# Third group of m's columns in the accumulators' banks, six g pairs parked in float32, and a maximum over partitions without a diagonal

## The chip, the cores and the metric

The program runs on one core of one Trainium2 chip. The metric is device time in microseconds of one execution of the whole program; smaller is better. The core has five engines that run at the same time, each through its own instruction list in order: TensorE (PE, matmuls; its weight loads are shown as PEld), VectorE (DVE), ScalarE (ACT), GpSimd (POOL) and SyncE (SP), which here only issues DMAs. They wait for each other by semaphores.

## The reference

```python
# q, k, v: (1, 6016, 256); tau = 1; C = 256, N = 6016
qn = q / (norm(q, axis=1) + 1e-6);  kn = k / (norm(k, axis=1) + 1e-6)
s = kn.transpose(0, 2, 1) @ qn / tau            # 256 x 256, contracted over the 6016 rows
a = softmax(s)                                  # over the last axis
x = v @ a                                       # 6016 x 256
h = x @ moe_w_in                                # 6016 x 2048
g = h * sigmoid(1.702 * h)
x = g @ moe_w_out                               # 6016 x 256
gate = sigmoid(x @ w_gate);  val = x @ w_val    # 6016 x 1536 each
out = (gate * val) @ moe2_w_out                 # 6016 x 256
```

The weights come as float64.

## The kernel before, in words

Everything is computed transposed: columns of v, h, g and y run along the free axis in 12 blocks of 512 tokens (the last one is shorter).

**Head of the program.** q and k are read in chunks; PE adds up the 256 x 256 scores in banks 0 and 1 of PSUM, the two accumulator banks (`ACC_BANK`). The norms, the softmax and a transpose give `et`. The weight w_in (256 x 2048, tile `full_in`, in four pieces of 512 columns) is turned from float64 words into float32: ACT takes the magnitude (line 503) and a sign (521), DVE shifts it (509) and joins the low bits (515), and GpSimd multiplies the sign in (525); ACT sums squares of a piece between shift and join (481), from which the piece's scale comes. w_out (called o1, tile `big`) goes the same way, since `BY_POOL` names "in" and "o1".

**m.** Softmax and w_in are folded into one matrix m = a @ w_in. Its 2048 columns come in four groups of 512, each in two halves: `m_unit` issues two float32 products (`L942`; four instructions in the profile) into one bank; ACT writes the float16 high part (`L312`, m_t<-ps), DVE the low part (`L315`, m_t<-ps). The scale `rss` of both comes from the maximum of w_in over all partitions: `p2_ops` builds a 128 x 128 diagonal of each partition's own maximum (`L281`, eye_b), multiplies it by ones on PE (`L285`) and takes the maximum of a row on DVE (`L288`, p_win; p_v is the same for block 0 of v, p_wo for o1).

**h and g.** An h unit (b, u) is a pair of 128-row tiles of h for block b (u = 0 to 7). In blocks 0 and 1 it is 12 float16 matmuls of 512 columns (`eight`: three products for each of 2 x 2 blocks) into a pair of PSUM banks; from block 2 on it is seven half-size products (`seven`, line 1031), which need sums of blocks of m (`m_sums`). For blocks 0 and 1 ACT then takes the gelu of both banks into a float32 tile gf (`L1175`), ACT or DVE makes the float16 high part gh (`L312` or `L1192`), and DVE the low part gl (`L315`). The tile gf has three buffers. gh and gl have three buffers (names gh, gl), and steps 3 to 11 have nine more (`room()`, shown as s_t) in memory that the head no longer needs.

**y.** A y unit multiplies a pair's gh and gl by w_out (tile `wo`, in high and low parts made by `L312` and `L315`, wo<-big) and adds into the accumulator banks (`L1007` to `L1009` with wo). So h units can run before w_out is ready, and y units can't.

**Order.** `Plan.run` is a list scheduler in the build: each operation has a cost, a rank (its number plus `plan.delay`) and its dependencies, and the scheduler writes out each engine's list. `ax_pair` hands out two pairs of PSUM banks in turn (4 and 5, 6 and 7) to units of m and h units; banks 2 and 3 serve `p2_ops` and later the seven products, banks 0 and 1 the scores and later y. On the chip each engine keeps the written order whatever happens. The lines on m, h and y at the program's end are

```python
M_FIRST, M_EVERY = 4, 1
m_units(M_FIRST)
        if b == 0 and u % 2 == 0:
            m_units((u // 2 + 1) * CC - m_next)
        h_unit(b, u, x - NG if NG <= x < NG + n_slots else None)
        if b == 0 and u % M_EVERY == M_EVERY - 1:
            m_units(CC)
        queue.append(step)
        if len(queue) > LAG:
            y_unit(*queue.pop(0))
```

Of the kernel before, what the change touches and what calls it, by code (L numbers as in the profile page):

```python
# [9 lines left out]
F32 = mybir.dt.float32  # L10
# [6 lines left out]
P = 128  # L17
# [3 lines left out]
LAG = 2  # L21
M_FIRST, M_EVERY = 4, 1
SUMS_AT = (1, 0), (1, 2), (1, 4), (1, 6)
# [5 lines left out]
S_AT = (73, 75, 86, 97)  # L29
BY_POOL = ("in", "o1")  # L30
LOOSE = ("in", "o1", "g", "v", "o2")

V0_DELAY, O1_DELAY, O1_SPLIT, SUM_FIRST = -105, 80, -20, 60

# [130 lines left out]
def fused_kernel(ctx, tc, q, k, vt, tau, w_in, w_o1, w_g, w_v, w_o2, outt):  # L165
# [93 lines left out]
    def p2_ops(name, amax, r, w, pe, before=(), after=()):  # L259
# [19 lines left out]

        def diagonal(e):  # L280
            nc.vector.tensor_scalar_mul(eye_b, T["ident_b"], own)  # L281

        def rows(e):
            T[kp] = bank(kp)
            nc.tensor.matmul(T[kp][:, :P], T["ones_b"], eye_b, start=True, stop=True)  # L285

        def top(e):
            nc.vector.tensor_reduce(out=p2, in_=T[kp][:, :P], axis=AX.X, op=ALU.max)  # L288

        op(diagonal, ("dve", 0.13), r=[k_own, ("ident_b",)], w=[("eye_b",)], lone=True)  # L290
        op(rows, ("pe", 0.1), r=[("eye_b",)], w=[kp])
        op(top, ("dve", 0.2), r=[kp], w=[w], lone=True)
        return p2

    def s_ops(name, p2, r, w, after=(), top=TOP):
# [4 lines left out]
        return s  # L300

    eye_b = small.tile([P, P], BF16, name="eye_b")

# [238 lines left out]
    def w_max(name, after=()):  # L542
# [26 lines left out]
        elif w_src[name][1]:  # L569
# [76 lines left out]
    def prepare(e):  # L646
        first["ones"] = sm_p.tile([P, P], F32, name="ones")
        nc.vector.memset(first["ones"], 1.0)
        T["ones_b"] = small.tile([P, P], BF16, name="ones_b")
        nc.vector.tensor_copy(T["ones_b"], first["ones"])  # L650
        first["k"] = sm_p.tile([P, TACC, C], F32, name="kacc")
# [278 lines left out]
    def m_unit(u):  # L930
# [4 lines left out]
        if i == 0:  # L935
            m_banks[fg] = ax_pair()
        kp = m_banks[fg][i]
# [191 lines left out]

    def h_unit(b, u, slot):  # L1130
        n = blocks[b][1]
# [4 lines left out]
        if u == 0:  # L1136
# [11 lines left out]
            for x, fn in enumerate((scale, inverse, shift)):  # L1148
                op(fn, ("dve", 0.07), r=[("vp2", b), ("sgin",)] + ([sk] if x else []), w=[sk])
        kf = ring("gf")  # L1150

# [21 lines left out]
        def both(e):  # L1173
            T[kf] = t_p.tile([P, 2 * NB], F32, tag="gf", name="gf" + name)
            nc.scalar.activation(  # L1175
                out=T[kf].rearrange("p (x n) -> p x n", x=2)[:, :, :n], in_=pair_ap(kx, n), func=AF.Gelu_apprx_sigmoid,
                scale=T[sk][0],
            )
# [20 lines left out]
        if b < PLAIN:  # L1199
            op(both, ("act", 0.12 + 1.02 * f), r=[kx, ka, sk], w=[kf], after=[t_op])  # L1200
            r = [kf, sk]
        else:
            op(lambda e: act(e, 0), ("act", 0.12 + 0.51 * f), r=[kx, ka, sk, kf], w=[("gf0", name)], after=[t_op])
            op(lambda e: act(e, 1), ("act", 0.12 + 0.51 * f), r=[kf, ("val2", kf), sk], w=[("gf1", name)], after=[t_op])
            r = [kf, ("gf0", name), ("gf1", name), sk]
        op(hi, [("act", 0.14 + 0.93 * f), ("dve", 0.1 + 0.53 * f, GH_DVE)], r=r, w=[k_g],
           after=before_m if slot == 0 else ())
        op(lo, ("dve", 0.12 + 1.14 * f), r=r + [k_g], w=[("glo", name)])
        g_keys[b, u] = k_g

# [125 lines left out]
    for x, step in enumerate(steps):  # L1336
        b, u = step
        if b == 0 and u % 2 == 0:
            m_units((u // 2 + 1) * CC - m_next)
        h_unit(b, u, x - NG if NG <= x < NG + n_slots else None)  # L1340
        if b == 0 and u % M_EVERY == M_EVERY - 1:
            m_units(CC)
        if step in SUMS_AT:
            m_sums(SUMS_AT.index(step))
        queue.append(step)
        if len(queue) > LAG:
            y_unit(*queue.pop(0))
# [171 lines left out]
```

## Time and profile before

| | |
|---|---|
| median of 3 runs | 1055.97 us (1055.26 to 1057.82) |
| the profiled execution | 1055.93 us, of which the span from the first to the last instruction is 1053.8 us |
| PE busy | 1038.5 us (99%), 7169 matmuls |
| PEld / DVE / ACT / POOL busy | 715.5 / 795.1 / 703.1 / 39.5 us (68% / 75% / 67% / 4%) |
| mean granted TensorE clock | 0.998 |
| share of PE in the chain that ended last | 92% |

Busy time is the sum of the instructions' times on an engine; a matmul's recorded time includes the passage of its last columns, so that neighbours overlap and a busy PE may still not be at its peak. The chain that ended last is followed back from the last instruction through whatever released each step. The three runs lie within 0.25% of each other.

### The profile page before, as it was taken

Reading aid. Unit: us, or ns where it says so; the run is one execution under the profiler, and the core shown is the slowest. Engines: PE = TensorE matmul, PEld = TensorE weight load, DVE = VectorE, ACT = ScalarE, POOL = GpSimd, SP = SyncE. Lnnn points to the kernel's source line nnn. Section 1 sums busy time; section 2 is a strip of 40 time slices with the busy share of each in tenths; the row PEclk is TensorE's granted clock in tenths of the full one; section 3 lists DMA queues with packets and bytes.
Section 4 is the critical chain, followed back from the end, with each engine's and each line's share of the span. In section 5 each row is a group of like instructions: output and inputs, shape, how many; then the busy total and the mean of one; then the engine's idle time right before and its main releaser. Section 6 shows DMA issues by size and latency. Waiting matters only on the chain.

```text
span 1053.8 us, 18271 instructions
## 1 busy us (share of the span) xinstructions
PE 1038.5 (99%) x7169; PEld 715.5 (68%) x7169; DVE 795.1 (75%) x1457; ACT 703.1 (67%) x1388; POOL 39.5 (4%) x43
## 2 busy tenths in 40 slices
PE   8989999999999999999999999999999999999998
PEld 6733456666666666666677777777777777777776
DVE  6988989989898766757686776767767667676665
ACT  6788467777867656656566666666666666666665
POOL 0232000000000000000000000000000000000000
PEclk9999999999999999999999999999999999999999
DMA  9930213210000000000000000000000000000000
GB/s 344 401 103 21 81 40 140 101 60 22 21 1 21 21 1 16 1 2 1 2 1 2 21 2 21 16 7 21 2 21 21 1 21 1 22 21 2 21 21 16
DMA packets 14518, 43.64 MB, mean 41 GB/s; under 512 B 1504, under 2 KB 2784, under 8 KB 12768
## 3 DMA queue, kind: packets, MB, share of 16 engines
q1 hardware_dynamic: 14432, 42.47, 11.2%
q8 instruction: 56, 0.92, 0.4%
q14 instruction: 30, 0.25, 0.1%
HBM read 36.31 MB, written 6.16 MB: 40 GB/s over the span
## 4 chain that ended last, share of the span: by engine, by line
PE 92%; DVE 2%; issue 2%; DMA 2%; ACT 1%; POOL 1%; SPq 0%; DVEq 0%; ACTq 0%; POOLq 0%
PE ps L1031 47%; PE ps L1009 14%; PE ps L1007 14%; PE ps L1008 14%; DMA m_t<-in_q 2%; PE ps L942 1%; PE ps L745 0%; POOL big L525 0%; DVE full_in L515 0%; POOL full_in L525 0%; PE ps L682 0%; DVE big L515 0%; DVE m_t L315 0%; ACT gh L312 0%; ACT m_t L1040 0%
## 5 line engine op out<-in xcount | busy, mean ns | idle before, releaser
L1031 PE MATMUL ps<-vo,s_t 128*128 128x256 f16 (+1 forms) x3024 | 371.0, 270 | 0.6 <-ACT m_t L1040 0.6
L1031 PEld LDWEIGHTS <-s_t 128*128 128x128 f16 x3024 | 292.7, 98 | 91.2 <-issue 1.0
L1045 DVE TENSOR_TENSOR gf<-ps,m_t 128x256 f32<-128x256 f32 (+1 forms) x448 | 184.8, 415 | 143.5 <-PE ps L1031 104.4
L1040 ACT COPY m_t<-ps 128x256 f32<-128x256 f32 (+1 forms) x448 | 162.3, 364 | 94.8 <-PE ps L1031 93.5
L1031 PE MATMUL ps<-vo,m_t 128*128 128x256 f16 (+1 forms) x1680 | 217.4, 270 | 0.4 <-ACT ps L1040 0.2
L1031 PEld LDWEIGHTS <-m_t 128*128 128x128 f16 x1680 | 162.6, 98 | 67.4 <-issue 1.5
L1393 ACT ACTIVATE gf<-ps,sgb 128x512 f32<-128x512 f32 (+1 forms) x144 | 97.5, 677 | 67.3 <-PE ps L1031 67.3
L1411 DVE TENSOR_TENSOR gl<-gf,gh 128x512 f16<-128x512 f32 (+1 forms) x144 | 97.8, 680 | 45.1 <-ACT gh L1406 42.4
L1009 PE MATMUL ps<-gh,wo 128*128 128x512 f16 (+1 forms) x348 | 130.2, 374 | 0.7 <-DVE wo L315 0.7
L1007 PE MATMUL ps<-gh,wo 128*128 128x512 f16 (+1 forms) x348 | 130.2, 374 | 0.7 <-ACT wo L312 0.7
L1008 PE MATMUL ps<-gl,wo 128*128 128x512 f16 (+1 forms) x348 | 130.2, 374 | 0.0
L1406 ACT CAST gh<-gf 128x512 f16<-128x512 f32 (+1 forms) x131 | 79.8, 609 | 72.0 <-PE ps L1009 71.8
L315 DVE SCALAR_TENSOR_TENSOR gl<-gf,sgi,gh 128x1024 f16<-128x1024 f32 (+1 forms) x87 | 110.2, 1269 | 4.0 <-ACT gh L312 3.6
L1399 DVE SCALAR_TENSOR_TENSOR gf<-gf 128x512 f32<-128x512 f32 (+1 forms) x144 | 98.0, 680 | 13.6 <-ACT gf L1393 0.7
L1008 PE MATMUL ps<-gl,wo_h 128*128 128x512 f16 (+1 forms) x288 | 107.9, 375 | 0.0
L1009 PE MATMUL ps<-gh,wo_l 128*128 128x512 f16 (+1 forms) x288 | 107.9, 375 | 0.0
L1007 PE MATMUL ps<-gh,wo_h 128*128 128x512 f16 (+1 forms) x288 | 107.9, 375 | 0.0
L1040 ACT COPY ps<-ps 128x256 f32<-128x256 f32 (+1 forms) x224 | 82.0, 367 | 16.8 <-PE ps L1031 15.7
L1192 DVE TENSOR_SCALAR gh<-gf,sgi 128x1024 f16<-128x1024 f32 (+1 forms) x64 | 49.0, 768 | 27.6 <-PE ps L1009 22.0
L1009 PEld LDWEIGHTS <-wo 128*128 128x128 f16 x384 | 37.6, 98 | 44.7 <-DVE wo L315 1.2
L1169 ACT ACTIVATE gf<-gf,sgs 128x512 f32<-128x512 f32 (+1 forms) x80 | 56.2, 709 | 14.4 <-DVE gf L1045 13.6
L1169 ACT ACTIVATE gf<-ps,sgs 128x512 f32<-128x512 f32 (+1 forms) x80 | 53.8, 673 | 11.1 <-PE ps L1031 10.7
(212 smaller groups left out, 999.7 us busy)
## 6 DMA issues: line engine op xcount, KB each, us to landing
v_raw<-in_vt SPq DMA_DIRECT2D x11, 512.0 KB, 3.9
out_t<-ob SPq DMA_DIRECT2D x22, 256.0 KB, 2.0
m_t<-in_k SPq DMA_DIRECT2D x9, 512.0 KB, 7.2
m_t<-in_q SPq DMA_DIRECT2D x9, 512.0 KB, 8.0
s_t<-in_w_o SPq DMA_DIRECT2D x3, 1024.0 KB, 4.9
s_t<-in_w_g SPq DMA_DIRECT2D x3, 1024.0 KB, 4.8
s_t<-in_w_v SPq DMA_DIRECT2D x3, 1024.0 KB, 4.9
big<-in_w_in SPq DMA_DIRECT2D x2, 1024.0 KB, 9.1
```

The lines of the kernel that those rows point to most:

```text
L315: nc.vector.scalar_tensor_tensor(out=lo, in0=x, scalar=s, in1=h, op0=ALU.mult, op1=ALU.subtract)
L1007: nc.tensor.matmul(ps[:, :n], w_h, x_h, start=first, stop=False)
L1008: nc.tensor.matmul(ps[:, :n], w_h, x_l, start=False, stop=False)
L1009: nc.tensor.matmul(ps[:, :n], w_l, x_h, start=False, stop=last)
L1031: nc.tensor.matmul(dst, l, r, start=start and y == 0, stop=y == 2, skip_group_check=True)
L1040: op(lambda e: nc.scalar.copy(out=dst, in_=bank(key)[:, :w]), ("act", 0.1 + w / 1150), r=[key], w=[wk], after=after)
L1045: nc.vector.tensor_add(val(half), bank(kw)[:, :w], other)
L1169: nc.scalar.activation(out=dst, in_=pair_ap(kx, w) if x == 0 else dst, func=AF.Gelu_apprx_sigmoid, scale=T[sk][0])
L1393: nc.scalar.activation(out=T[kf][:, :n].rearrange("p (x w) -> p x w", x=2), in_=pair_ap(kx, w), func=AF.Sigmoid, scale=T[sk])
L1399: nc.vector.scalar_tensor_tensor(out=v, in0=v, scalar=VSHIFT, in1=T[kf][:, :n], op0=ALU.mult, op1=ALU.mult)
L1406: nc.scalar.copy(out=T[name][0][:, :n], in_=T[kf][:, NB : NB + n])
L1411: nc.vector.tensor_sub(T[name][1][:, :n], T[kf][:, NB : NB + n], T[name][0][:, :n])
```

## The change

Four edits, and what follows from them in the written order.

1. **Banks of m.** Six units of m are issued ahead of the first h unit instead of four (`M_FIRST`), and the third group (fg == 2) goes to the accumulator banks 0 and 1 instead of a pair from `ax_pair`. The maximum of o1 moves from bank 0 to bank 3.
2. **Parked g.** For six h units, steps 3 to 8, that is (0,3) to (0,7) and (1,0), the gelu is written into float32 space of the late tiles y_f, wo_h and wo_l (`parked`) instead of the gf buffers; the high and low parts of these have a rank that is 60 later (`PARK_BY`).
3. **The maximum.** The diagonal and the tile of ones go. The own maximum of each partition, read as bfloat16 and broadcast along the columns, is the weight operand, and the identity is multiplied by it.
4. **o1 without GpSimd, and ranks.** o1 leaves `BY_POOL`: its sign is now joined by a second DVE operation (line 512 in the new file) in place of ACT's sign (521) and GpSimd's product (525), for each of four pieces. The maximum, scale and split of v's block 1 get a rank 60 earlier (`V1_DELAY`), and each `m_sums` stands behind the first product of its step.

```diff
-M_FIRST, M_EVERY = 4, 1
+M_FIRST, M_EVERY = 6, 1
...
-BY_POOL = ("in", "o1")
+BY_POOL = ("in",)
...
+V0_DELAY, V1_DELAY, O1_DELAY, O1_SPLIT, SUM_FIRST = -105, -60, 80, -20, 60
+PARK, PARK_BY = 6, 60
...
-        def diagonal(e):
-            nc.vector.tensor_scalar_mul(eye_b, T["ident_b"], own)
-
         def rows(e):
+
             T[kp] = bank(kp)
-            nc.tensor.matmul(T[kp][:, :P], T["ones_b"], eye_b, start=True, stop=True)
+            left = own.bitcast(BF16)[:, 1:2].broadcast_to([P, P])
+            nc.tensor.matmul(T[kp][:, :P], left, T["ident_b"], start=True, stop=True)
...
-            {"in": ("acc", 3), "o1": ("acc", 0)}.get(name), before, after,
+            {"in": ("acc", 3), "o1": ("acc", 3)}.get(name), before, after,
...
         if i == 0:
-            m_banks[fg] = ax_pair()
+
+            m_banks[fg] = ACC_BANK if fg == 2 else ax_pair()
...
+    def parked(i):
+
+        if i < YX:
+            return late_pools()["y"][:, i * 2 * NB : (i + 1) * 2 * NB]
+        return late_pools()["o2"][i - YX].bitcast(F32)[:, : 2 * NB]
...
-        kf = ring("gf")
+        kf = ring("gf") if park is None else ("gfp", park)
...
-            T[kf] = t_p.tile([P, 2 * NB], F32, tag="gf", name="gf" + name)
+            T[kf] = t_p.tile([P, 2 * NB], F32, tag="gf", name="gf" + name) if park is None else parked(park)
...
+        plan.delay = 0 if park is None else PARK_BY
         op(hi, [("act", 0.14 + 0.93 * f), ("dve", 0.1 + 0.53 * f, GH_DVE)], r=r, w=[k_g],
...
-        h_unit(b, u, x - NG if NG <= x < NG + n_slots else None)
+        h_unit(b, u, x - NG if NG <= x < NG + n_slots else None, x - NGF if NGF <= x < NGF + PARK else None)
...
-            m_sums(SUMS_AT.index(step))
+            m_sums(SUMS_AT.index(step), [step_op[step]])
...
+            plan.delay = V1_DELAY if b == 0 and fn in (v_max, v_scale, v_split) else 0
             fn(*args, after=[step_op[step]])
+            plan.delay = 0
```

On PE, from the transposes' end to the first h unit, the order before is this (two rows of `L942` are one unit of m; `own_v`, `own_win` and `eye_b` belong to the maxima of v's block 0 and of w_in):

```order
L942 MATMUL ps<-full_in,et 128x512 x6
L285 LDWEIGHTS ones_b
L285 MATMUL ps<-eye_b,ones_b 128x128
L942 MATMUL ps<-full_in,et 128x512 x2
L285 LDWEIGHTS ones_b
L285 MATMUL ps<-eye_b,ones_b 128x128
L942 MATMUL ps<-full_in,et 128x512 x2
L1007 LDWEIGHTS m_t
```

and this is the order of the changed kernel at the same place:

```order
L938 MATMUL ps<-full_in,et 128x512 x6
L285 LDWEIGHTS own_win
L285 MATMUL ps<-ident_b,own_win 128x128
L938 MATMUL ps<-full_in,et 128x512 x6
L1003 LDWEIGHTS m_t
```

Six units of m now stand ahead of the first h unit instead of five, and v's maximum has left this place: its matmul stands ahead of the last filler matmuls, before the transposes.

On DVE, around the softmax's row sums (se, rs), the order before has the shifts (`L509`) and the join (`L515`) of w_in's pieces and then the chain to w_in's maximum (wpm_in to own_win):

```order
L898 RECIPROCAL rs<-se_584 128x1
L509 TENSOR_SCALAR full_in<-full_in 128x2x512
L897 TENSOR_SCALAR se_589<-se_589 128x1
L898 RECIPROCAL rs<-se_589 128x1
L509 TENSOR_SCALAR full_in<-full_in 128x2x512
L515 SCALAR_TENSOR_TENSOR full_in<-wo_87,full_in 128x2x512
L546 TENSOR_REDUCE wpm_in<-sums_in 128x1
```

and the changed kernel has there (s_v and vo are the scale and the low part of v's block 0):

```order
L842 TENSOR_REDUCE nm_584<-sc_579 128x1
L892 TENSOR_SCALAR se_582<-se_582 128x1
L893 RECIPROCAL rs<-se_582 128x1
L288 TENSOR_REDUCE p_v_105<-ps 128x1
L297 RECIPROCAL s_v_106<-p_v_105 128x1
L892 TENSOR_SCALAR se_587<-se_587 128x1
L893 RECIPROCAL rs<-se_587 128x1
L297 TENSOR_SCALAR s_v_106<-s_v_106 128x1
L506 TENSOR_SCALAR full_in<-full_in 128x2x512 x2
L312 SCALAR_TENSOR_TENSOR vo<-v_raw_485,s_v_106,vo 128x1024
L512 SCALAR_TENSOR_TENSOR full_in<-wo_87,full_in 128x2x512
L543 TENSOR_REDUCE wpm_in<-sums_in 128x1
```

The scale and the low part of v's block 0 now stand ahead of the join of w_in's third piece and of that chain. On ACT, v's high part stands ahead of the last two sums of squares of w_in.

A little later on DVE, from w_in's maximum p_win to the first low parts of m, the order before is

```order
L288 TENSOR_REDUCE p_win<-ps 128x1
L298 RECIPROCAL s_win<-p_win 128x1
L298 TENSOR_SCALAR s_win<-s_win 128x1
L904 TENSOR_SCALAR rss<-rs,s_win 128x2
L912 TENSOR_SCALAR i_in<-p_win 128x1
L914 TENSOR_SCALAR sg_in<-i_in 128x1
L281 TENSOR_SCALAR eye_b<-ident_b,own_v_105 128x128
L515 SCALAR_TENSOR_TENSOR full_in<-raw_in_526,full_in 128x2x512
L288 TENSOR_REDUCE p_v_106<-ps 128x1
L298 RECIPROCAL s_v_107<-p_v_106 128x1
L298 TENSOR_SCALAR s_v_107<-s_v_107 128x1
L315 SCALAR_TENSOR_TENSOR m_t<-ps,rss,m_t 128x2x256 x3
```

and of the changed kernel

```order
L288 TENSOR_REDUCE p_win<-ps 128x1
L297 RECIPROCAL s_win<-p_win 128x1
L297 TENSOR_SCALAR s_win<-s_win 128x1
L899 TENSOR_SCALAR rss<-rs,s_win 128x2
L907 TENSOR_SCALAR i_in<-p_win 128x1
L909 TENSOR_SCALAR sg_in<-i_in 128x1
L512 SCALAR_TENSOR_TENSOR full_in<-raw_in_523,full_in 128x2x512
L1142 TENSOR_SCALAR sgs_646<-p_v_105,sg_in 128x1
L312 SCALAR_TENSOR_TENSOR m_t<-ps,rss,m_t 128x2x256 x6
```

The diagonal, the maximum and the scale of v have left the stretch between p_win and the low parts of m; ahead of it, the diagonal of own_win is gone too. The low parts of m stand in one run of six.

On GpSimd, from w_in's third piece to the maximum of v's block 1 (p_v), the order before is

```order
L525 TENSOR_TENSOR full_in<-full_in,wo_87 128x2x512
L525 TENSOR_TENSOR full_in<-full_in,raw_in_526 128x2x512
L525 TENSOR_TENSOR big<-big,wo_87 128x1024
L525 TENSOR_TENSOR big<-big 128x1024
L275 ISA
L275 ISA p_v_117<-own_v_116 128x1
L525 ISA
L525 TENSOR_TENSOR big<-big 128x1024
L525 TENSOR_TENSOR big<-big,wo_87 128x1024
```

and of the changed kernel

```order
L522 TENSOR_TENSOR full_in<-full_in,big 128x2x512
L522 TENSOR_TENSOR full_in<-full_in,wo_87 128x2x512
L522 TENSOR_TENSOR full_in<-full_in,raw_in_523 128x2x512
L276 ISA
L276 ISA p_v_116<-own_v_115 128x1
```

The four products of o1 have left GpSimd. On DVE four more operations of line 512 (big<-big or big<-wo) stand between the low parts of the first h units. On PE, nine h units stand ahead of the matmul of o1's maximum (`L285`, own_wo) in both orders; between it and the first y unit there is one h unit before, (1,1), and now there are two, (1,1) and (1,2).

## Rows read from the trace of the kernel before

**Rows 1.** The page: span, busy times, and DVE's line for gh (mean ns behind the comma).

```profile
span 1053.8 us, 18271 instructions
...
PE 1038.5 (99%) x7169; PEld 715.5 (68%) x7169; DVE 795.1 (75%) x1457; ACT 703.1 (67%) x1388; POOL 39.5 (4%) x43
...
L1192 DVE TENSOR_SCALAR gh<-gf,sgi 128x1024 f16<-128x1024 f32 (+1 forms) x64 | 49.0, 768 | 27.6 <-PE ps L1009 22.0
```

**Rows 2.** Stretches (us): length, busy PE, PEld, DVE, ACT, POOL; PEclk, DMA share, GB/s.

```profile
60.00:70.00 10.00, 6.39 (x15) 2.24 (x15) 8.94 (x22) 8.12 (x11) 2.38 (x1) 0.83 0.49 157
60.00:110.00 50.00, 43.93 (x174) 18.71 (x174) 44.90 (x66) 39.08 (x44) 12.38 (x6) 0.97 0.13 42
110.00:240.00 130.00, 129.69 (x789) 77.02 (x788) 118.55 (x199) 90.96 (x150) 5.52 (x8) 1.00 0.25 86
110.00:1050.00 940.00, 938.93 (x6761) 654.75 (x6759) 701.01 (x1301) 618.04 (x1285) 16.88 (x25) 1.00 0.06 22
```

**Rows 3.** Who PE waited for: total us, times, longest.

```profile
PE ps L942 <- DVE m_t L315: 3.6, 1, 3.6
...
PE ps L285 <- DVE eye_b L281: 1.1, 1, 1.1
PE ps L1009 <- DVE wo L315: 0.7, 1, 0.7
PE ps L1007 <- ACT wo L312: 0.7, 1, 0.7
```

**Rows 4.** PE in order of time, 59.7 to 71.5: start, us, instruction, idle before.

```profile
59.76 1.93 PE L942 MATMUL ps<-full_in,et 128*128 128x512 f32 x4
61.53 0.22 PE L285 MATMUL ps<-eye_b,ones_b 128*128 128x128 bf16 x1
65.36 2.99 PE L942 MATMUL ps<-full_in,et 128*128 128x512 f32 x4 [3.61 <-DVE m_t L315]
68.15 0.63 PE L1007 MATMUL ps<-vo,m_t 128*128 128x512 f16 x1
...
71.44 1.02 PE L942 MATMUL ps<-full_in,et 128*128 128x512 f32 x2
```

**Rows 5.** DVE in order of time, 55.9 to 66.5.

```profile
55.90 1.24 DVE L515 SCALAR_TENSOR_TENSOR full_in<-wo,full_in 128x1024 uint32<-128x1024 uint32 x1 [0.90 <-ACT junk L481]
...
58.02 1.63 DVE L281 TENSOR_SCALAR eye_b<-ident_b,own_win 128x128 bf16<-128x128 bf16 x1
59.96 0.29 DVE L288 TENSOR_REDUCE p_win<-ps 128x1 f32<-128x128 f32 x1 [0.31 <-PE ps L285]
...
61.06 0.24 DVE L281 TENSOR_SCALAR eye_b<-ident_b,own_v 128x128 bf16<-128x128 bf16 x1
...
63.15 2.07 DVE L315 SCALAR_TENSOR_TENSOR m_t<-ps,rss,m_t 128x512 f16<-128x512 f32 x3
65.13 1.27 DVE L315 SCALAR_TENSOR_TENSOR vo<-v_raw,s_v,vo 128x1024 f16<-128x1024 f32 x1
```

**Rows 6.** GpSimd in order of time, three of its products.

```profile
57.21 2.39 POOL L525 TENSOR_TENSOR full_in<-full_in,wo 128x1024 f32<-128x1024 f32 x1 [3.62 <-DVE full_in L515]
...
96.16 2.48 POOL L525 TENSOR_TENSOR big<-big 128x1024 f32<-128x1024 f32 x1 [7.07 <-ACT gf L1175]
98.60 2.39 POOL L525 TENSOR_TENSOR big<-big,wo 128x1024 f32<-128x1024 f32 x1
```

**Rows 7.** DVE's groups, shapes kept apart, 60 to 110: busy us, mean ns, idle before.

```profile
L315 DVE SCALAR_TENSOR_TENSOR s_t<-gf,sgi,s_t 128x1024 f16<-128x1024 f32 x5 | 7.6, 1516 | 0.0
...
L315 DVE SCALAR_TENSOR_TENSOR gl<-gf,sgi,gh 128x1024 f16<-128x1024 f32 x3 | 5.2, 1740 | 0.0
L315 DVE SCALAR_TENSOR_TENSOR wo<-big,s_wo,wo 128x1024 f16<-128x1024 f32 x4 | 4.9, 1280 | 0.1
...
L515 DVE SCALAR_TENSOR_TENSOR big<-wo,big 128x1024 uint32<-128x1024 uint32 x2 | 2.4, 1224 | 1.1 <-ACT junk L481 1.1
...
L281 DVE TENSOR_SCALAR eye_b<-ident_b,own_wo 128x128 bf16<-128x128 bf16 x1 | 1.6, 1642 | 0.0
```

More of the change, by code (lines that the diff above doesn't have):

```diff
@@ L29 @@
 S_AT = (73, 75, 86, 97)
-BY_POOL = ("in", "o1")
+BY_POOL = ("in",)
 LOOSE = ("in", "o1", "g", "v", "o2")
-V0_DELAY, O1_DELAY, O1_SPLIT, SUM_FIRST = -105, 80, -20, 60
+V0_DELAY, V1_DELAY, O1_DELAY, O1_SPLIT, SUM_FIRST = -105, -60, 80, -20, 60
+PARK, PARK_BY = 6, 60
 POOL_PEN, GH_DVE = -0.3, 0.3
@@ L278, in p2_ops @@
         kp = pe
-        def diagonal(e):
-            nc.vector.tensor_scalar_mul(eye_b, T["ident_b"], own)
         def rows(e):
             T[kp] = bank(kp)
-            nc.tensor.matmul(T[kp][:, :P], T["ones_b"], eye_b, start=True, stop=True)
+            left = own.bitcast(BF16)[:, 1:2].broadcast_to([P, P])
+            nc.tensor.matmul(T[kp][:, :P], left, T["ident_b"], start=True, stop=True)
         def top(e):
             nc.vector.tensor_reduce(out=p2, in_=T[kp][:, :P], axis=AX.X, op=ALU.max)
-        op(diagonal, ("dve", 0.13), r=[k_own, ("ident_b",)], w=[("eye_b",)], lone=True)
-        op(rows, ("pe", 0.1), r=[("eye_b",)], w=[kp])
+        op(rows, ("pe", 0.1), r=[k_own, ("ident_b",)], w=[kp])
         op(top, ("dve", 0.2), r=[kp], w=[w], lone=True)
@@ L300, in s_ops @@
         return s
-    eye_b = small.tile([P, P], BF16, name="eye_b")
     def tiny(fns, r, w, after=(), costs=None):
@@ L648, in prepare @@
         nc.vector.memset(first["ones"], 1.0)
-        T["ones_b"] = small.tile([P, P], BF16, name="ones_b")
-        nc.vector.tensor_copy(T["ones_b"], first["ones"])
         first["k"] = sm_p.tile([P, TACC, C], F32, name="kacc")
@@ L1128, in eight, with h_unit @@
         return *keys, ops[0]
-    def h_unit(b, u, slot):
+    def parked(i):
+        if i < YX:
+            return late_pools()["y"][:, i * 2 * NB : (i + 1) * 2 * NB]
+        return late_pools()["o2"][i - YX].bitcast(F32)[:, : 2 * NB]
+    def h_unit(b, u, slot, park=None):
         n = blocks[b][1]
@@ L1199, in h_unit @@
         if b < PLAIN:
-            op(both, ("act", 0.12 + 1.02 * f), r=[kx, ka, sk], w=[kf], after=[t_op])
+            op(both, ("act", 0.12 + 1.02 * f), r=[kx, ka, sk], w=[kf], after=[t_op] + (before_m if park == 0 else []))
             r = [kf, sk]
@@ L1348, in fused_kernel @@
         for fn, args in side.pop(step, ()):
+            plan.delay = V1_DELAY if b == 0 and fn in (v_max, v_scale, v_split) else 0
             fn(*args, after=[step_op[step]])
+            plan.delay = 0
     assert not side, side
```

## The prediction

> **What bounds the kernel now.** I read the page first. PE is busy for 99% of the span [rows 1], so time can come only from the holes in PE's line, from stretches in which its clock is low, or from fewer matmuls, and the change leaves the products as they are. The stretches show where the holes are: from 110 to 1050 us PE idles for 940 - 938.9 = 1.1 us, but from 60 to 110 us for 50 - 43.9 = 6.1 us, and the granted clock, 1.00 elsewhere, is 0.83 from 60 to 70 [rows 2]. PE's waits name the holes: 3.6 us of a unit of m (L942) for DVE's low part of m, 1.1 for the diagonal of o1's maximum, 0.7 and 0.7 for the high and low part of w_out [rows 3].
>
> The first hole, in order of time [rows 4]: PE is through four units of m at 61.53 and starts the fifth at 65.36. That unit takes a bank that an earlier unit of m used, and DVE's third low part (63.15 + 2.07 = 65.22) frees it [rows 5]. DVE is late because p_win came only at 59.96, behind a diagonal of 1.63 us, and because a diagonal, a join and v's maximum stand between p_win and the low parts. After the hole PE is slow: the fifth unit takes 68.15 - 65.36 = 2.79 us where the fourth took 61.53 - 59.76 = 1.77, and the first h unit takes 71.44 - 68.15 = 3.29 us where 12 x 512 columns at 2.4 GHz are 2.56. The clock fell to its lower level of 1.2 GHz behind the idle stretch: the mean of 0.83 is a third of 10 us at half.
>
> The second hole is w_out. Its last GpSimd product ends at 98.60 + 2.39 = 100.99 [rows 6], and only then does ACT start the high parts. GpSimd costs DVE too: the same diagonal takes 0.24 us alone and 1.63 beside a GpSimd product, with its end (59.65) on that product's end (57.21 + 2.39 = 59.60) [rows 5, 6].
>
> **The change, part by part.** The sum is made against the profiled execution, 1055.93 us (span 1053.8, 2.1 around it), 0.04 below the median of 1055.97; what comes off the span comes off both.
>
> *Banks, v ahead, no diagonal: the first hole.* With the accumulator banks two units of m need nobody's bank: PE goes on from 61.53 and is through six units at 61.53 + 2 x 1.77 = 65.07. Is everything there? v's high and low part (1.2 to 1.3 us each, taken from the low part's 1.27 [rows 5]) now stand ahead of the third piece's join, one on ACT, one on DVE behind it, so the join moves from 55.90 to about 57.3 and the chain behind it 1.4 us later. The diagonal of 1.63 falls out of the same chain, so p_win stays near 59.9. The join's GpSimd product moves from 57.21 to 58.6 and ends at 61.0, 0.5 ahead of the fifth unit, which needs it. DVE then has six small operations (to 61.1), one join (1.22 [rows 7]), a scale (0.2) and the low parts at 0.69 each: the two that the first h unit needs are ready at about 64.0 to 64.3, because ACT's high parts come after two magnitudes that moved ahead. v is ready long before. So PE runs through and keeps its clock. Saved: the hole from start to start, 65.36 - 61.53 - 0.05 = 3.78 (0.05 is the small matmul between, 128 columns at 2.4 GHz); the slow unit, 2.79 - 1.77 = 1.02; the slow h unit, 3.29 - 2.56 = 0.73. Together 5.5 us.
>
> *o1 without GpSimd: the second hole.* Four joins are added on DVE, 4 x 1.22 = 4.9 us, four products leave GpSimd, four signs leave ACT. In 60 to 110 DVE is busy 44.9 of 50 us [rows 2], so 4.9 us more would not fit. But the products also stretched DVE: three gl at 1.74 instead of 1.27 (1.4 us), five parked low parts s_t at 1.52 (1.2 us), two gh at 1.69 instead of 0.77 (1.8 us), and two diagonals of 1.64 and 0.24 go (1.9 us) [rows 1, 5, 7]. That is 6.3 us off against 4.9 on: DVE ends about 1.4 us lighter.
>
> Here the Trainium skill speaks against the edit: Perfetto Trace Analysis, section Optimizing Scalar/DVE Operations, says that where DVE is saturated, giving work to ScalarE or even GpSimd may make sense, though it warns that GpSimd shares a port with DVE. The edit goes the other way; by the first half of that rule the 4.9 us would stand in PE's way and leave 7.7 - 4.9 = 2.8 us, by the rows the stretching weighs more.
>
> *Parked g.* The six gelus have the same size and engine, written elsewhere: nothing by itself. Their low parts (6 x 1.27 = 7.6 us) move behind the joins, so o1's maximum comes sooner. PE needs 65.07 + 2 units of m (3.5) + 9 h units (9 x 2.57, by the 12 x 512 columns) = 91.7 until own_wo's matmul. DVE, counted from 61.1 along its new order: nine joins 11.0, eight low parts of m 5.5, four shifts at 0.7, five low parts of g and v 6.4, two gh 1.5, a maximum 1.2, some 20 small ones 2 to 3, in all about 30.5: 91.6, less some 0.07 by which neighbours overlap. So own_wo is there when PE is, give or take 1 us; before, PE waited for it [rows 3]. Then PE has two h units (5.2 us) where it had one. In them DVE has the maximum's two steps, a sum of m, a parked low part and the first w_out low part (1.28), and ACT the high part: about 5 us, just in time. The waits removed are 1.1 + 0.7 + 0.7 = 2.5 us [rows 3], and a wait is some 0.17 longer from start to start than as listed (3.78 against 3.61 in the first hole), so 3.0 us.
>
> *Behind the parked low parts* queue sums of m, v's block 2 and the y units of (0,5) onwards. PE reaches these at about 110 us; DVE is then through them by some 5 us. That is the cover; without it each costs PE up to 1.27.
>
> *At nothing:* the tile of ones (a cast in the first microsecond, where PE waits for loads), the broadcast weight load (no row of a broadcast exists; the nearest, a weight load of ones, is within the 0.22 of its matmul, so below 0.3 for three either way), the bank of o1's maximum, and the ranks of v's block 1, which move a maximum that DVE does anyway.
>
> **Sum.** 5.5 + 3.0 = 8.5 us. Three places are ready within 0.2 to 0.7 us (fifth unit, own_wo, first w_out part), and the order of everything behind is new; I take 0.8 us of new waits. 8.5 - 0.8 = 7.7; 1055.97 - 7.7 = **1048.3 us**. Without the allowance it is 1047.5, with 2 to 3 us of waits up to 1050.5.
>
> **Rivals.**
> 1. *DVE takes part of it back later.* PE comes 8.5 us sooner to 110 us, DVE only about 6. From 110 to 240 DVE is busy 118.6 of 130 us [rows 2]. If PE then waits for sums of m, v's split or a gl, 2.4 to 5 us go: 1049.9 to 1052.5. For it: so little slack. Against: PE waited for nothing there before.
> 2. *The joins are paid in full,* because the stretching was in DVE's slack: 4.9 us back, 1048.3 + 4.9 = 1053.2. Against: the stretched diagonal of o1 stood directly in PE's way [rows 3].
> 3. *The first hole stays* (the change doesn't do what it says): v's two operations ahead of the chain cost more than the diagonal, PE idles as before at the first h unit, the clock falls. Only 3.0 us and less come: 1053 to 1054.
> 4. *Slower.* The parked low parts starve PE: they all fall due when the first y units have used up what is ready. DVE's six low parts and four joins, 7.6 + 4.9 = 12.5 us, would have to reach PE whole: 12.5 - 8.5 = 4.0 us slower, 1060.0. It decides from the point where DVE's 11.4 us of slack in 110 to 240 [rows 2] are gone; I see no chain that long.
>
> **Chances.** Forecast (1046.6 to 1050.5) 0.62, rival 1 0.18, rival 2 0.08, rival 3 0.07, rival 4 0.05. The measurement tells about 0.3% from no change, that is 3.2 us: faster means below 1052.8. The forecast and nearly all of rival 1, with a part of 2 and 3, lie there: 0.84; same 0.11; slower 0.05. The range takes the forecast and rival 1 and ends at 1052.6; the forecast's own is 1046.6 to 1050.5.
>
> **What would show it.** First step right: no wait of L938 for a low part of m, the first h unit's first matmul near 65 us, granted clock 1.00 from 60 to 70. Wrong: a wait at the first L1003, or p_win after 61. Second step right: no DVE row of gl above 1.4 us, own_wo's matmul near 92 us, first y matmul near 97, PE's idle time in 60 to 110 below 1.5 us. Rival 1 shows as PE waits for DVE behind 110 us; then that term, and not the first two, was wrong.

## The result, and the profile after

The changed kernel takes 1046.91 us (median of 5 runs, 1046.38 to 1047.54); the kernel before, run beside it, 1056.41. The ratio is 0.9907, with a 95% interval of 0.9897 to 0.9918: 0.93% or some 9.8 us faster (9.5 between these two medians), where 7.7 were forecast. The median lies 0.3 us above the low end of the predicted range; the ratio applied to the 1055.97 us that stood at the head of the prediction gives 1046.2, which is 0.4 below it.

The first place to look at is who PE waited for. Columns as in [rows 3]:

```profile
PE ps L740 <- DMA m_t<-in_q: 2.2, 2, 1.2
PE ps L677 <- POOL idle L653: 1.3, 1, 1.3
PE ps L867 <- ACT ex L847: 1.3, 2, 1.0
PE ps L755 <- DVE kacc L720: 0.6, 1, 0.6
PE ps L1027 <- ACT m_t L1036: 0.6, 1, 0.6
```

All four lines of [rows 3] are gone and none has come in their place; what is left lies in the head and far behind. The stretches (columns as in [rows 2]) say the same:

```profile
60.00:70.00 10.00, 10.00 (x31) 4.42 (x30) 9.14 (x22) 9.30 (x13) 4.12 (x2) 1.00 0.44 157
60.00:110.00 50.00, 50.00 (x213) 22.49 (x212) 47.33 (x75) 40.61 (x47) 6.94 (x4) 1.00 0.13 42
110.00:240.00 130.00, 130.00 (x814) 79.48 (x813) 121.14 (x212) 92.93 (x159) 5.65 (x9) 1.00 0.24 86
```

PE is busy for 50.00 of 50 us where it was 43.93, for 130.00 of 130 where it was 129.69, and its clock stays at 1.00. PE in order of time (start, us, instruction; units of m, first h units, the two maxima, the first y unit):

```profile
55.25 5.39 PE L938 MATMUL ps<-full_in,et 128*128 128x512 f32 x12
60.48 0.22 PE L285 MATMUL ps<-ident_b,own_win 128*128 128x128 bf16 x1
60.53 5.37 PE L938 MATMUL ps<-full_in,et 128*128 128x512 f32 x12
65.74 0.38 PE L1003 MATMUL ps<-vo,m_t 128*128 128x512 f16 x1
...
92.48 0.22 PE L285 MATMUL ps<-ident_b,own_wo 128*128 128x128 bf16 x1
...
97.72 0.38 PE L1003 MATMUL ps<-gh,wo 128*128 128x512 f16 x1
```

The first unit of m starts 0.93 us later than before (55.25 against 54.32). From the matmul of the norms' sums (46.26 before, 47.20 after) to it both take 8.1 us, so the difference lies ahead of that, where PE waits for loads: 1.3 us before, 2.2 after. Over the profiles of this study the first unit of m starts between 54.3 and 55.5. (One profile, that of the kernel with the old rank of v's block 1, was taken in a run of 1081.28 us at a granted clock of 0.95 and is not used.) I take the difference as the loads' chance; since the kernel before and its two variants start at 54.3 to 54.6 and the changed kernel's at 54.5 to 55.5, a small part that belongs to the change is not excluded. So I compare profiles from the first unit of m to the end of the span: 1053.8 - 54.32 = 999.5 us before, 1045.7 - 55.25 = 990.5 after, 9.0 less. Nearly all of it is ahead of the first half-size product, up to which both kernels have the same matmuls but for v's small one (0.05 us), which now stands ahead of m: 144.56 - 54.32 = 90.24 before, 136.57 - 55.25 = 81.32 after, 8.9 less.

Two things more separate these 9.0 us from the 9.5 to 9.8 of the runs. The time of an execution less its span is some 2.1 us in every run of the kernel before and some 1.8 in every run of the changed kernel: 0.3 us of the gain lie outside the instructions, and the profile does not show why. (The other programs of this study have 1.8 too, but for the one with w_in off GpSimd, which has 2.4.) And the profiled execution of the changed kernel, 1047.52, lies 0.6 above its median, that of the kernel before, 1055.93, 0.5 below. Between these two it is 9.0 - 0.9 + 0.3 = 8.4 us, and with the 0.6 and 0.5 it is the 9.5 of the medians.

On DVE and GpSimd the places that could have been late, in order of time:

```profile
60.74 0.29 DVE L288 TENSOR_REDUCE p_win<-ps 128x1 f32<-128x128 f32 x1 [0.67 <-PE ps L285]
...
63.23 4.19 DVE L312 SCALAR_TENSOR_TENSOR m_t<-ps,rss,m_t 128x512 f16<-128x512 f32 x6
...
90.69 0.15 DVE L269 TENSOR_SCALAR own_wo<-cl_wo 128x1 uint32<-128x1 uint32 x1
...
96.05 4.87 DVE L312 SCALAR_TENSOR_TENSOR wo<-big,s_wo,wo 128x1024 f16<-128x1024 f32 x4 [0.24 <-ACT wo L309]
...
59.33 2.39 POOL L522 TENSOR_TENSOR full_in<-full_in,wo 128x1024 f32<-128x1024 f32 x1 [4.80 <-DVE wpm_in L543]
63.26 2.39 POOL L522 TENSOR_TENSOR full_in<-full_in,raw_in 128x1024 f32<-128x1024 f32 x1 [1.53 <-ACT m_t L309]
```

The third piece of w_in is there when its product ends, at 59.33 + 2.39 = 61.72, and the fifth unit of m, which needs it, starts at 60.53 + 1.74 = 62.27 (a unit takes (65.74 - 60.53) / 3 = 1.74); the first two low parts of m are through at 63.23 + 2 x 0.70 = 64.6 and needed at 65.74 at the earliest; own_wo is there at 90.84 and needed at 92.48; the first low part of w_out ends at 97.33 and is needed by the third y matmul at 98.15. The margins are 0.55, 1.1, 1.6 and 0.8 us. And DVE's groups of 60 to 110 us (columns as in [rows 7]) have lost their stretching:

```profile
L312 DVE SCALAR_TENSOR_TENSOR s_t<-y_f,sgi,s_t 128x1024 f16<-128x1024 f32 x4 | 5.1, 1276 | 0.0
...
L312 DVE SCALAR_TENSOR_TENSOR gl<-gf,sgi,gh 128x1024 f16<-128x1024 f32 x3 | 3.8, 1273 | 0.0
...
L1194 DVE TENSOR_SCALAR gh<-gf,sgi 128x1024 f16<-128x1024 f32 x2 | 1.5, 746 | 0.0
```

Means of 1.28, 1.27 and 0.75 us stand where [rows 7] and the trace of before had 1.52, 1.74 and 1.69.

### The profile page after: what moved, and what is told of

Its sections match the earlier page's. It is cut to its first block, busy times and chain, and to the rows that moved or that the text cites. A ratio compares the mean times of both kernels' runs of the same rounds, so it can differ in the third digit from the quotient of the medians.

```text
span 1045.7 us, 18259 instructions
## 1 busy us (share of the span) xinstructions
PE 1035.7 (99%) x7169; PEld 715.4 (68%) x7169; DVE 789.1 (75%) x1454; ACT 699.6 (67%) x1387; POOL 31.4 (3%) x39
## 4 chain that ended last, share of the span: by engine, by line
PE 93%; DVE 2%; issue 2%; DMA 1%; ACT 1%; POOL 0%; SPq 0%; ACTq 0%; POOLq 0%
PE ps L1027 47%; PE ps L1005 15%; PE ps L1004 15%; PE ps L1003 15%; PE ps L938 1%; DMA big<-in_w_in 1%; DMA m_t<-in_q 0%; PE ps L740 0%; SPq L703 0%; POOL full_in L522 0%; DVE s_t L312 0%; DVE gl L312 0%; DVE full_in L512 0%; DVE big L627 0%; ACT gh L309 0%
## 5 line engine op out<-in xcount | busy, mean ns | idle before, releaser
L1399 ACT ACTIVATE gf<-ps,sgb 128x512 f32<-128x512 f32 (+1 forms) x144 | 97.6, 678 | 66.5 <-PE ps L1027 66.5
L1412 ACT CAST gh<-gf 128x512 f16<-128x512 f32 (+1 forms) x132 | 80.4, 609 | 71.5 <-PE ps L1005 71.3
L1194 DVE TENSOR_SCALAR gh<-gf,sgi 128x1024 f16<-128x1024 f32 (+1 forms) x62 | 45.7, 738 | 27.3 <-PE ps L1005 25.1
```

Of the source, the lines that this page charges most:

```text
L1399: nc.scalar.activation(out=T[kf][:, :n].rearrange("p (x w) -> p x w", x=2), in_=pair_ap(kx, w), func=AF.Sigmoid, scale=T[sk])
L1412: nc.scalar.copy(out=T[name][0][:, :n], in_=T[kf][:, NB : NB + n])
```

## The experiments

My theory was the prediction's: two holes, each closed by its own edits, and the GpSimd products lengthen DVE's work by more than the four joins cost. The rivals: one edit did all of it; joins and stretching cancel; the two savings don't simply add up. Each run stands beside runs of the kernel before on its chip, so the ratios compare. "From m" is the profile's time from the first unit of m to the end of the span, worked out as above.

| run | median us | ratio to before (95%) | from m, us |
|---|---|---|---|
| before | | 1 | 999.5 |
| changed | 1046.91 | 0.9907 (0.9897 to 0.9918) | 990.5 |
| changed, banks undone | 1049.04 | 0.9929 (0.9915 to 0.9942) | 992.5 |
| changed, o1 on GpSimd | 1054.08 | 0.9976 (0.9966 to 0.9985) | 997.0 |
| changed, no parking | 1052.38 | 0.9959 (0.9946 to 0.9971) | 995.1 |
| changed, diagonal, its own order | 1049.27 | 0.9931 (0.9919 to 0.9944) | 992.4 |
| changed, diagonal, same order | 1049.01 | 0.9931 (0.9919 to 0.9943) | 992.3 |
| changed, idle GpSimd products | 1050.61 | 0.9946 (0.9934 to 0.9958) | 993.9 |
| changed, three parked | 1046.92 | 0.9907 (0.9893 to 0.9920) | 990.1 |
| changed, w_in off GpSimd too | 1048.56 | 0.9925 (0.9912 to 0.9939) | 991.2 |
| changed, old rank of v's block 1 | 1047.24 | 0.9912 (0.9899 to 0.9926) | |
| changed, old rank of the sums | 1047.53 | 0.9913 (0.9900 to 0.9927) | 990.5 |
| before, banks alone | 1060.88 | 1.0040 (1.0028 to 1.0052) | 1004.5 |
| before, o1 off GpSimd alone | 1058.12 | 1.0015 (1.0006 to 1.0023) | 1001.3 |

### One edit undone in the changed kernel

**Banks.**

```diff
-            m_banks[fg] = ACC_BANK if fg == 2 else ax_pair()
+            m_banks[fg] = ax_pair()
```

> The changed kernel, in which only the third group of m goes back to a pair of banks from ax_pair (still six units ahead of the first h unit). My theory (the bank was what PE waited for): PE is ready for the fifth unit at about 62.3 us in the changed kernel's trace, and the first low part, which now frees its bank, ends there at 63.9, so PE waits about 1.8 us, and 1046.9 becomes about 1048.8; if the granted clock falls behind that wait as it did before, up to 1.8 more, 1050.5. Rival (the shorter chain on DVE closed the first hole and the banks do nothing): no wait of L938 for a low part, 1046.9.

PE in order of time, of the kernel with the banks undone:

```profile
63.34 3.67 PE L938 MATMUL ps<-full_in,et 128*128 128x512 f32 x8 [1.65 <-DVE m_t L312]
```

The wait is back in its old place, and it costs 2.0 us from m on (1049.04 where 1048.8 was expected). It is shorter than the 3.6 of [rows 3]: PE goes on 0.2 us behind the end of the first low part (it starts at 62.44 and takes 0.70), where before it was the third that freed the bank. The clock stayed at 1.00 behind it. So the bank is a cause, but only some 2 of the first hole's 5.5 us hang on it once the rest is in place.

**o1 back on GpSimd.**

```diff
-BY_POOL = ("in",)
+BY_POOL = ("in", "o1")
```

> The changed kernel, in which o1 alone goes back to GpSimd (BY_POOL names in and o1 again). My theory (the products stretch DVE more than the four joins cost, and the last product ends late): DVE rows of gl, gh or s_t of 2.4 us or more come back beside the products, w_out is late again, PE waits 1 to 3 us at own_wo's matmul and the first y units: 1048 to 1050. Rival (by the rule that a saturated DVE should be relieved by GpSimd): four joins of 1.22 us less on DVE leave it 4.9 us lighter, no wait, 1046.9 or less.

It is worse than I expected: 6.5 us from m on. PE's waits of this kernel:

```profile
PE ps L1003 <- ACT wo L309: 2.8, 1, 2.8
...
PE ps L1005 <- DVE wo L312: 0.9, 1, 0.9
PE ps L1003 <- ACT y_f L1177: 0.8, 1, 0.8
```

And its GpSimd, ACT and DVE in order of time:

```profile
81.63 3.47 POOL L522 TENSOR_TENSOR big<-big,wo 128x1024 f32<-128x1024 f32 x1 [7.02 <-ACT y_f L1177]
85.06 2.84 POOL L522 TENSOR_TENSOR big<-big 128x1024 f32<-128x1024 f32 x1
...
94.38 3.36 POOL L522 TENSOR_TENSOR big<-big,wo 128x1024 f32<-128x1024 f32 x1 [1.22 <-ACT s_t L309]
...
97.78 4.27 ACT L309 ACTIVATE wo<-big,s_wo 128x1024 f16<-128x1024 f32 x4 [1.92 <-POOL big L522]
...
82.76 5.70 DVE L506 TENSOR_SCALAR big<-big 128x1024 uint32<-128x1024 uint32 x2
```

Two shifts that take 0.68 us each alone stand for 5.70 us, from 82.76 to 88.46: until both GpSimd products are done (85.06 + 2.84 = 87.90) and then 0.56 more. The product that began beside a join took 3.47 instead of 2.39. Each blocks the other. The last product starts at 94.38 here and ends at 97.74, and ACT starts the first high part of w_out, which waits for it, at 97.78. The rival by which GpSimd relieves DVE is out: with 4.9 us of joins less, DVE was later (own_wo is there 36.6 us behind the first unit of m, 35.6 in the changed kernel). Behind the 2.8 us wait the clock was at 0.83 from 100 to 110 us, and that is part of the 6.5.

**No parking.**

```diff
-PARK, PARK_BY = 6, 60
+PARK, PARK_BY = 0, 60
```

> The changed kernel without parking (PARK = 0): the six gelus go to the three gf buffers again, and their high and low parts keep their old rank. My theory: five low parts of 1.27 us stand ahead of o1's maximum on DVE again, 6.4 us; in the changed kernel own_wo is ready 1.6 us before PE comes to it, so DVE is 4.8 us late, less what PE finds in h units that the order puts ahead (it holds two more): 2 to 5 us of waits of PE, 1049 to 1052. Rival (parking only moves work that is hidden anyway): no new wait, 1046.9.

The stretch in which PE waited, of this kernel (columns as in [rows 2]):

```profile
90.00:100.00 10.00, 6.93 (x28) 2.54 (x27) 9.21 (x20) 5.84 (x6) 0.35 (x1) 0.88 0.00 1
```

4.6 us from m on (1052.38, just above the upper end of what I expected). The wait, 2.8 us for the first high part of w_out and 0.3 for the low part, is where the theory has it, and about 1 us of the loss is the clock, which the expectation had left out.

**The diagonal.** Two kernels: one in which the planner sees the diagonal as an operation of its own, as before (its order then moves v's maximum back too), and one with every other instruction in the changed kernel's order, whose edit is

```diff
-            left = own.bitcast(BF16)[:, 1:2].broadcast_to([P, P])
-            nc.tensor.matmul(T[kp][:, :P], left, T["ident_b"], start=True, stop=True)
+            nc.vector.tensor_scalar_mul(eye_b, T["ident_b"], own)
+            nc.tensor.matmul(T[kp][:, :P], T["ones_b"], eye_b, start=True, stop=True)
```

> The changed kernel with the diagonal and the tile of ones again in the three maxima over partitions. My theory: w_in's diagonal stands beside the third GpSimd product and is stretched to about 1.6 us again, so p_win and all low parts come 1.6 us later; the second low part was ready 1.1 us before the first h unit needed it, so PE waits about 0.5 us there, and 0.2 at o1's: 1047.5. Rival A (the diagonal was the main cause of the first hole): PE waits 3 us or more and the clock falls, 1050 to 1052. Rival B (it costs 0.24 us and nothing waits): 1046.9.

> The changed kernel with the diagonal and the matmul by ones in the three maxima, but with every other instruction in the changed kernel's order. My theory: w_in's diagonal meets the GpSimd product that starts at 59.3 us there and ends at 61.7, so p_win comes 1.3 us later and PE waits 0.3 to 0.6 us at the first h unit; 0.2 more in the softmax and nothing at o1's maximum: 0.5 to 0.9 above the changed kernel, about 1047.6. Rival A (what cost 2 us with the diagonal in the other order was the diagonal): 1049. Rival B (it is free): 1046.9.

Both cost some 2.5 us by their ratios and 1.8 to 1.9 from m on, more than my theory gave either; 1049.01 is rival A's value for the second. PE, DVE and GpSimd in order of time, of the kernel with the same order:

```profile
61.51 0.22 PE L285 MATMUL ps<-eye_b,ones_b 128*128 128x128 bf16 x1 [1.18 <-DVE eye_b L284]
...
59.79 1.67 DVE L284 TENSOR_SCALAR eye_b<-ident_b,own_win 128x128 bf16<-128x128 bf16 x1
...
59.02 2.39 POOL L524 TENSOR_TENSOR full_in<-full_in,wo 128x1024 f32<-128x1024 f32 x1 [4.95 <-DVE wpm_in L545]
```

The length was right (1.67 us, up to the product's end at 61.41), the place was wrong. I looked for the wait at the first h unit, who reads what is late; it is at the maximum's own small matmul, which stands in PE's list between the third and the fourth unit of m and holds up all that is queued behind it: 1.3 of the 1.8 us are gone by the first h unit, and where the rest goes, behind the first half-size product, is open. In the kernel with its own order v's low part stands behind w_in's maximum again, the diagonal comes 1.2 us sooner and that matmul meets no wait; there 0.4 us go at the units of m and the rest later, whose cause is open too.

### One edit alone in the kernel before

```diff
-M_FIRST, M_EVERY = 4, 1
+M_FIRST, M_EVERY = 6, 1
...
-            m_banks[fg] = ax_pair()
+            m_banks[fg] = ACC_BANK if fg == 2 else ax_pair()
...
-            {"in": ("acc", 3), "o1": ("acc", 0)}.get(name), before, after,
+            {"in": ("acc", 3), "o1": ("acc", 3)}.get(name), before, after,
```

> The kernel before, with the first edit alone (six units of m first, the third group in the accumulator banks, o1's maximum in bank 3). My theory (the two holes are one behind the other: what PE saves at the first it waits for at w_out, whose GpSimd products and stretched DVE operations come at nearly the same time as before): the first hole of 3.6 us is gone and the clock stays at 1.00 there, but the waits for w_out grow from 2.5 us to 4 to 6; in all 1 to 3 us faster than the kernel before beside it. Rival (the two savings add up as in the sum of the prediction): the whole 5.5 us of the first hole less 0.5 for the diagonal, about 5 us faster.

```diff
-BY_POOL = ("in", "o1")
+BY_POOL = ("in",)
```

> The kernel before, with o1 alone taken off GpSimd (BY_POOL names in only), so four more joins on DVE and no parked g. My theory: the first hole stays as it is (3.6 us), DVE's stretched operations of 60 to 110 us are gone, and with the 4.9 us of joins and all low parts of g still ahead of the maximum w_out comes no sooner than before: within 1.5 us of the kernel before. Rival A (the stretching was worth more than the joins by itself): the second hole closes, 2.5 to 3 us faster. Rival B (the joins are paid in full): 3 to 5 us slower.

Both come out slower than the kernel before: by 4.2 us and by 1.6, the second just beyond the 1.5 that I gave. My theory of the first had the right sense (what is saved at the first hole is waited for later), but far too small a size: I expected a gain of 1 to 3 us. The longest waits of PE in the kernel with the banks alone:

```profile
PE ps L1007 <- ACT gf L1175: 3.8, 1, 3.8
PE ps L1007 <- ACT wo L312: 2.0, 1, 2.0
```

And its GpSimd, ACT and DVE in order of time:

```profile
76.58 3.38 POOL L525 TENSOR_TENSOR big<-big,wo 128x1024 f32<-128x1024 f32 x1 [11.26 <-DVE cl_v L265]
85.89 0.38 POOL L275 PARTITION_ALL_REDUCE p_v<-own_v  x1 [5.94 <-issue]
...
86.69 1.15 ACT L312 ACTIVATE vo<-v_raw,s_v 128x1024 f16<-128x1024 f32 x1 [2.21 <-DVE s_v L298]
...
77.61 2.90 DVE L1192 TENSOR_SCALAR gh<-gf,sgi 128x1024 f16<-128x1024 f32 x1
...
86.30 0.16 DVE L298 RECIPROCAL s_v<-p_v 128x1 f32<-128x1 f32 x1 [3.28 <-POOL p_v L275]
```

The first h unit starts 12.9 us behind the first unit of m, with seven units of m done, where it was 13.8 with five: the first hole is closed. But the maximum of v's block 1 still waits for GpSimd, which stands for 5.94 us between a product and this all-reduce (5.99 in the kernel before, nearly hidden there). Now that PE is early, the others stand at it: DVE for 3.28 us at the scale, ACT for 2.21 at v's high part, both lists in order, and the gelus behind v's high part free PE's banks 3.8 us late. With the clock at 0.88, 0.78 and 0.83 of full speed in the three stretches of 10 us from 80 to 110 us that is more than the hole was worth. In the kernel with o1 alone off GpSimd the first hole stays (a wait of 3.6 us), and w_out is waited for 2.8 + 0.3 us: the joins and the low parts of g stand ahead of the maximum together, and the clock falls behind both waits. Parking alone and the new maximum alone, in the kernel before, were not run.

### GpSimd beside DVE, measured by itself

The changed kernel; the orders of PE, DVE, ACT and SP stay, and the second join of each of o1's four pieces is followed by two products on GpSimd whose result nobody reads:

```diff
+        def idle_products(i):
+            for x in range(2):
+                nc.gpsimd.tensor_mul(spare, part(name, 2 * i + x), part(name, 2 * i + x))
...
-            w_op(name, lambda e: join(0, ALU.logical_shift_right, 29), ("dve", 1.22), r=[kr, kw],
+            w_op(name, lambda e: (join(0, ALU.logical_shift_right, 29), name == "o1" and idle_products(i)), ("dve", 1.22), r=[kr, kw],
```

> The changed kernel with the same order on PE, DVE, ACT and SP, and behind each of o1's four joins two GpSimd products of 512 columns (about 1.2 us each, 9.6 us in all) whose result nobody reads. My theory (a DVE operation that comes while a GpSimd product runs stands still until the product ends, and the other way round): single DVE operations between 78 and 95 us are 0.5 to 2.4 us longer, 4 us or more in all, which is past the 1.6 us that o1's maximum had to spare, and PE waits 2 to 7 us: 1049 to 1054. Rival (GpSimd and DVE work side by side, and what made the kernel with o1 on GpSimd slow was its other order): no wait, 1046.9.

PE's waits for DVE in this kernel:

```profile
PE ps L286 <- DVE own_wo L270: 1.8, 1, 1.8
PE ps L1010 <- DVE wo L313: 1.4, 1, 1.4
```

And its GpSimd and DVE in order of time:

```profile
82.66 7.65 POOL L531 TENSOR_TENSOR spare<-big 128x512 bf16<-128x512 f32 x4 [7.51 <-DVE gl L313]
...
83.39 4.04 DVE L513 SCALAR_TENSOR_TENSOR big<-big 128x1024 uint32<-128x1024 uint32 x2
87.35 2.06 DVE L513 SCALAR_TENSOR_TENSOR big<-wo,big 128x1024 uint32<-128x1024 uint32 x1
```

The two joins take 4.04 us where the changed kernel has 2.35 at the same place, the next 2.06 instead of 1.22. PE waits 3.2 us and the kernel loses 3.5 from m on. This settles the disputed step with no change of order on any other engine: work on GpSimd that nothing waits for slows the path through DVE.

### Smaller edits and margins

```diff
-PARK, PARK_BY = 6, 60
+PARK, PARK_BY = 3, 60
```

> The changed kernel with three parked g pairs instead of six. On DVE one more low part (1.27 us) then stands ahead of o1's maximum and two more between it and w_out's first low part. My theory (the slack read from the changed kernel's trace is real: 1.6 us at o1's maximum, some 0.8 at the first low part of w_out): no wait at the maximum, about 0.8 us at the first low part of w_out, 1047.7. Rival A (only full parking helps): 1052, as without parking. Rival B (half of it is enough): 1046.9.

No wait, and no difference to six: rival B. The margin of 0.8 us at w_out's first low part held what moved there (that part now starts at 96.58 and ends at 97.85, needed at 98.03).

```diff
-BY_POOL = ("in",)
+BY_POOL = ()
```

> The changed kernel with w_in off GpSimd too (BY_POOL empty). My theory (a GpSimd product is bad only where DVE is on the path beside it, and w_in's joins would stand on DVE ahead of the first low parts of m): the low parts come 2 to 3 us later, PE waits 0.5 to 2 us at the first h unit, 1047.4 to 1049. Rival (each GpSimd product taken away helps): no wait and a shorter softmax, 1045 to 1046.

As my theory has it in sign, 0.7 us from m on, but not in place: PE waits 0.9 us for a later low part of m, at 76.49, and 0.5 more in the softmax than the changed kernel. Of the 1.9 us by the ratio 0.6 lie outside the span (2.4 us in these runs, 1.8 in the changed kernel's). GpSimd is worth its price for w_in, by about 1 us.

```diff
-V0_DELAY, V1_DELAY, O1_DELAY, O1_SPLIT, SUM_FIRST = -105, -60, 80, -20, 60
+V0_DELAY, V1_DELAY, O1_DELAY, O1_SPLIT, SUM_FIRST = -105, 0, 80, -20, 60
```

> The changed kernel with V1_DELAY = 0: the maximum, scale and split of v's block 1 keep their old rank. The prediction put this edit at nothing: 1046.9, within 0.7. Rival (the four joins now come ahead of block 1's split, and PE comes sooner to its first unit than before): PE waits 1 to 3 us for vo at the first h unit of block 1, 1048 to 1050.

```diff
-            m_sums(SUMS_AT.index(step), [step_op[step]])
+            m_sums(SUMS_AT.index(step))
```

> The changed kernel with the sums of m where they stood (not behind the first product of their step). Only two operations of DVE change places around o1's maximum (1.22 and 0.42 us). The prediction named no price: 1046.9, within 0.7, since the maximum has 1.6 us to spare. Rival: the two stand ahead of the maximum and PE waits about 0.5 us or more at its matmul or at the first y unit, 1047.4 or more.

The ratios of these two, 0.9912 and 0.9913, lie within the interval of the changed kernel: nothing that can be told.

## Why the prediction was right and wrong

**The first hole: right, a little small.** Before, the first h unit came 68.15 - 54.32 = 13.83 us behind the first unit of m with five units done; now it comes 10.49 behind it with six. Before, five units at (65.74 - 60.53) / 3 = 1.74, start to start, and two small matmuls are 8.8, so 5.0 us of hole and slow unit are gone, and 0.7 of the slow h unit: 5.7, where the sum had 5.5. p_win came at 60.74, less the 0.93 of the head 59.8, where 59.9 was said; the join's GpSimd product ended 0.55 ahead of the fifth unit, where 0.5 was said.

**The second hole: right.** own_wo's matmul at 92.48, less 0.93 at 91.55, where 91.7 was said; two h units behind it, no wait. From start to start the three waits of [rows 3] were worth 1.24 + 0.83 + 0.87 = 2.9 us, and two holes of 0.1 that no view lists bring it to 3.1, where the sum had 3.0.

**The step that failed: "I take 0.8 us of new waits".** None came. The sum without it was 8.5; the trace shows 9.0. The fifth unit was ready 0.55 us ahead, within the 0.2 to 0.7 that I gave all three places, but own_wo and w_out's first low part were ready 1.6 and 0.8 ahead. The largest error is own_wo's: I added DVE's operations to 91.6 and found it just in time. It was there at 90.84, on the clock of before at 89.9. The rows' durations overlap (two joins in a row take 2.35 us, not 2.44): DVE's 44 operations from 61.91 to 90.84 add up to 31.1 us and take 28.9, with 3.0 us of overlap and 0.8 of gaps, and I had taken off 0.07 once. From that too pessimistic a margin came the allowance, and the low end of the range stood only 0.9 below the bare sum, while the head alone scatters by 1.1.

**A second, smaller step failed: "what comes off the span comes off both".** The 2.1 us outside the span, which the sum held fixed, became 1.8 in every run of the changed kernel. No term had these 0.3 us, and their cause stays open. With the 0.8 of the allowance and the 0.5 by which the holes were larger than their terms they make 1.6 of the 2.1 us between 7.7 and the measured 9.8; the remaining 0.5 is no more than the interval of the ratio, 1.1 us to either side.

**The stretching: right.** gl, s_t and gh went to 1.27, 1.28 and 0.75 us. The rule that I weighed against it (the Trainium skill, Perfetto Trace Analysis, section Optimizing Scalar/DVE Operations) would, by its first half, have DVE relieved by GpSimd; the runs with o1 on GpSimd and with the idle products bear out its second half, the warning about the shared port, at 6.5 and 3.5 us.

**Rivals.** DVE took nothing back behind 110 us: PE is busy there for 130.00 of 130. The joins were not paid in full, the first hole did not stay, and the parked low parts starved nothing. But what rival 1 names, time saved early and waited for later, is what the banks do alone: 4.2 us slower.

**What I had not seen** is that the terms were no terms of the single edits. Undone one at a time in the changed kernel, banks, o1, parking and diagonal cost 2.0, 6.5, 4.6 and 1.8 us from m on, 14.9 together, for a gain of 9.0: each leaves a place late, and twice the clock falls there too. Banks or o1 alone, in the kernel before, lose. As I read it, the sum came out nearly right because it was made of PE's holes, with all of the change in place, and not of the edits' own savings. The ranks of v's block 1 and of the sums, put at nothing, could not be told from nothing.

## What to carry to other kernels

Where one engine is busy for 99%, make the sum from its holes and ask of the whole change only whether each place is ready in time; a package of edits can gain where one of them alone loses, because an early engine meets the next late one. Work out readiness from start to start in the trace, not from added durations, and leave the allowance out where the margins come out above the error of that sum. In a list that is kept in order, look for the wait at the first instruction that needs the late value, however small it is, and not at its largest user; and move work to GpSimd only where DVE, beside it, is not on the path.

## What the runs showed of the hardware

**DVE and GpSimd shut each other out by whole instructions, and only for some shapes.** Beside GpSimd products two shifts (TENSOR_SCALAR on 128x1024; o1 on GpSimd), a join (idle products), a gl (the kernel before, from 81.13) and a diagonal (same order) took 5.70, 2.06, 2.67 and 1.67 us instead of 1.29, 1.22, 1.27 and 0.24, and each ended at a product's end or behind it. The low parts of m were not touched: six of them take 4.19 us, 0.70 each, beside a product from 63.26 to 65.65 in the changed kernel. They read PSUM (the matmuls' banks) and one operand in SBUF (the memory of the other tiles), the others two operands in SBUF or one in a simple TENSOR_SCALAR. The Trainium skill (SBUF — State Buffer, section Who interferes with whom) has this as a lock on a shared port pair that the second to issue waits for, and counts a DVE instruction with two SBUF inputs among those that want it and one with at most one, outside the two-port modes, among those that don't; the rows with two SBUF inputs and the low parts of m agree. Whether the TENSOR_SCALARs that waited run in a two-port mode no trace here shows.

**GpSimd stood idle for 5.9 us or more at every change seen here between a product and an all-reduce.** It stood for 5.94 us ahead of the all-reduce in the kernel with the banks alone, with nothing in the profile that it waited for, for 5.99 in the kernel before, and for 7.51 between an all-reduce and the first of the idle products, whose join was done 4.5 us before it began. In the changed kernel it goes from products to all-reduces once, in 8.9 us that no other engine waits for.

**The clock fell behind the longer waits.** Behind PE's waits of 2.8 us (o1 on GpSimd, no parking, o1 alone), 3.6 (before, o1 alone) and 3.8 (banks alone) it fell from 2.4 to 1.2 GHz, and the stretches of 10 us in which it fell read 0.78 to 0.88; it fell once more behind waits of 1.1, 2.0 and 0.7 us close together (banks alone, from 99 to 105 us). Behind single waits of 1.6 and 1.8 (banks undone, idle products), and behind 1.1, 0.7 and 0.7 close together (before), it read 1.00. So waits of 2.8 and 0.3 us cost 4.6 in one kernel, and one of 1.6 us 2.0 in another.
